# Attention and a gated feed-forward layer on one core: a written-out order of all tasks, other engines for some, and 32-column matmuls for one batch's kv

## The chip, the core and the metric

The kernel runs on one core of one Trainium2 chip. The metric is the time of one execution in device microseconds (us). The core has five engines that each work through their own list of instructions in order and wait for one another through semaphores: TensorE (PE in the profile, with its weight loads as PEld), VectorE (DVE), ScalarE (ACT), GpSimd (POOL) and SyncE (SP), whose queue issues the transfers here.

## What is computed

Four batches of attention with four heads, 1088 positions and 32 elements a head, by a polynomial feature map, then a normalized, gated feed-forward layer over all 4352 tokens:

```python
def phi(x):                                     # r = 8: 64 features of a head
    a = np.einsum('rd,bhsd->bhsr', S1, x)
    b = np.einsum('rd,bhsd->bhsr', S2, x)
    return np.einsum('bhsi,bhsj->bhsij', a, b).reshape(*x.shape[:-1], r * r)
q_p, k_p = phi(q), phi(k)
kv  = np.einsum('bhsf,bhsd->bhfd', k_p, v)      # one 64 x 32 matrix of a batch and head
z   = np.sum(k_p, axis=2)
num = np.einsum('bhsf,bhfd->bhsd', q_p, kv)
den = np.einsum('bhsf,bhf->bhs', q_p, z)[..., None] + 1e-06
x   = (num / den)                               # as 4352 tokens x 128
xn  = x / np.sqrt(np.mean(x * x, axis=-1, keepdims=True) + 1e-06) * rms_g
g, val = xn @ w_gate, xn @ w_val                # 128 -> 1536
out = g * (1 / (1 + np.exp(-g))) * val @ w_out  # 1536 -> 128
```

The weights and the sketch matrices S1 and S2 arrive as 64-bit floats, and the kernel converts them to 32 bits itself.

## The kernel before

**Tiling.** The 4352 tokens are cut into nine chunks, eight of 512 and one of 256. The 1536 hidden features are cut into twelve groups j of 128. A *slot* is one chunk and one j: gate product into `g_ps` and value product into `v_ps` (L786), silu on ScalarE (L795, tile `s`), their product `h` on VectorE (L798), and the product back to 128 features, added up in `o_ps` over the twelve j (L822, or L805 for the first four slots and the last two). Chunks 0 and 1 go through j in two halves each, chunks 2 to 8 in one pass. Slots are numbered t = 0 to 107 in that order.

**Split numbers.** TensorE multiplies rounded 32-bit numbers (fp32r) in one pass. So weights and activations are split in a rounded high and a rest: `w_hi`, `w_lo` (L494, L497), `x_hi`, `x_lo` (L738, L741), `h_hi` on ScalarE (L813) and `h_lo` on VectorE (L816). Each product is three matmuls. L805 multiplies exact 32-bit numbers instead, which takes no split. Attention's matmuls are exact too.

**Weights.** For each j, 384 KB are loaded into `w_raw` (L486) and converted by five steps on VectorE, the first of which may go to ScalarE (L426 to L445), then split. L497 may go to VectorE or GpSimd.

**Keys** (`kside`, one batch each): `kt` is multiplied with the sketch matrix `sblk` (L570), the 64 features of each head are formed as products (L528, L531; for one group of batch 0 on GpSimd, L513), and `kv` is added up over nine tiles of 128 positions (L580), with z as a 33rd column. Both use half of the array's columns: 64 columns of output to a matmul, in two column groups.

**Queries** (`qside`, one chunk each): features for chunks 0 and 1 as for the keys (L624, L531), then transposed (L632). For later chunks they are multiplied (L651), sent out to memory and read back spread (`at`, `bt`), and multiplied on VectorE (L677). Then numerators and denominators (L693), the division (L711, L712, L703), the mean square (`sq` on ScalarE, L715, with a scaling on VectorE, L725), its root on GpSimd (L728), scaling (L731 or L749), transposing (L735) and the split.

**What sets the order.** All of this is first collected as 1252 tasks in a plan: a task has the tiles that it reads and writes, and for each engine that may do it a cost in ns. `forward` (L231) then plays the engines through: at each step it takes the engine that can start earliest and, of its open tasks, the one with the lowest `late`, a number for each task from the table `LATE`. On TensorE a task gets 4000 on top if it changes between exact and rounded (`KIND`, L290). A task that two engines can do goes to the one that would finish it first. The instructions are written in the order of the start times that come out, and each engine works through its own in that order. Where TensorE would be idle for over 400 ns in that play, small warming matmuls are put in (L420).

Task numbers, which the new table uses, run in the order in which the code adds tasks: 0 to 7 the sketch matrix, 8 to 33 keys of batch 0 (with the first queries' load), 34 to 65 queries of chunk 0, 66 the load of chunk 1's, 67 to 186 weights, ten tasks a j, 187 to 204 keys of batch 1, 205 to 231 queries of chunk 1, then the slots, eleven tasks each for t = 0 and 1 (232 to 253), five for 2 and 3 and seven for later ones, with the keys of batches 2 and 3 and the queries of later chunks in between.

Of the kernel before, what the change touches and what calls it, by code (L numbers as in the profile page):

```python
# [19 lines left out]
R = 8  # L20
F = R * R
NT = B * S
P = 128
# [19 lines left out]
VPIECES = [(0, 5), (5, 9)]  # L43
K0 = [(0, 1), (1, 4), (4, 6), (6, 9)]
KN = [(0, 3), (3, 6), (6, 9)]
HOP = {"act": 36, "dve": 34, "pool": 80, "pe": 54, "dma": 60}
FIRST = 15000
LEADS = 1, 1.5, 2, 3, 4
EACHES = 2150, 2300, 2400
TELL = False  # L50
LATE = """
# [48 lines left out]
"""  # L100
LOOK = 250
MARGIN = 1500
KIND = 4000
WRAW = 7
POOL_K, POOL_Q = (1,), ()
LO_POOL, SCALED_ACT, PUT_ACT = 600, 100, 0
# [806 lines left out]
```

## Time and profile before

| | |
|---|---|
| Time, median of 3 runs | 272.04 us (271.98 to 272.32) |
| Profiled execution | 272.2 us, its span 270.0 us |
| Instructions | 4975 |
| TensorE busy | 263.7 us, 1842 matmul records |
| VectorE busy | 201.0 us, 383 |
| ScalarE busy | 162.1 us, 385 |
| GpSimd busy | 23.2 us, 37 |
| Granted TensorE clock | 1.000 |
| HBM read, written | 18.69 MB, 3.08 MB |

The span runs from the first to the last instruction. A matmul of exact 32-bit numbers shows as two records. Matmuls overlap in the array, so a row's mean duration is longer than the distance from one to the next; the chain of waits, which gives the time until the next piece begins, shows that distance. "x24" is a count.

### The profile page before, as it was taken

The numbers are of one execution on the slowest core, as the hardware profiler recorded it, in microseconds if no ns is written. First come the engines' busy times: TensorE is split into PE (matmuls) and PEld (weight loads), VectorE is DVE, ScalarE is ACT, GpSimd is POOL, SyncE is SP. The second block draws the span as 40 slices with busy tenths as digits, with TensorE's granted clock in tenths as the row PEclk, the third lists the DMA queues.
The fourth block names the chain that finished last, engine by engine and source line by source line (L and its number), as shares of the span: only waits on it lengthen the run. The fifth ranks groups of instructions, "written<-read, shape, count | busy, mean of one in ns | idle before, by whom it ended". The sixth has DMA issues, their size and how long they took to land.

```text
span 270.0 us, 4975 instructions
## 1 busy us (share of the span) xinstructions
PE 263.7 (98%) x1842; PEld 209.4 (78%) x1842; DVE 201.0 (74%) x383; ACT 162.1 (60%) x385; POOL 23.2 (9%) x37
## 2 busy tenths in 40 slices
PE   7899999999999999999999999999999999999995
PEld 4767687687788787778778787887777887887895
DVE  3799999999676786659646967678757755967582
ACT  4488796557554665717587556546646553855671
POOL 3132221230100010000100010001000100000000
PEclk9999999999999999999999999999999999999999
DMA  6999333041045001520016101610042001200100
GB/s 201 395 401 353 105 92 83 0 128 55 2 123 170 4 0 47 129 79 2 0 58 161 35 1 40 165 34 0 10 131 75 0 0 50 81 0 0 41 0 19
DMA packets 12087, 22.08 MB, mean 82 GB/s; under 512 B 1568, under 2 KB 3360, under 8 KB 12064
## 3 DMA queue, kind: packets, MB, share of 16 engines
q1 hardware_dynamic: 11920, 21.78, 25.5%
q8 instruction: 14, 0.23, 0.3%
q14 instruction: 9, 0.07, 0.1%
q10 hardware_dynamic: 144, 0.00, 0.0%
HBM read 18.69 MB, written 3.08 MB: 81 GB/s over the span
## 4 chain that ended last, share of the span: by engine, by line
PE 90%; DVE 4%; DMA 2%; ACT 1%; SPq 1%; issue 1%; POOL 0%; ACTq 0%
PE g_ps L786 26%; PE v_ps L786 26%; PE o_ps L822 24%; PE att L693 3%; PE att L580 3%; DMA vt<-v 2%; PE o_ps L805 2%; PE att L735 1%; PE att L651 1%; PE att L570 1%; PE o_ps L580 1%; DVE h L798 1%; DVE w_tmp L433 1%; DVE h_lo L816 0%; ACT h_hi L813 0%
## 5 line engine op out<-in xcount | busy, mean ns | idle before, releaser
L798 DVE TENSOR_TENSOR h<-v_ps,s 128x512 f32<-128x512 f32 (+2 forms) x109 | 70.1, 654 | 32.8 <-ACT s L795 16.1
L795 ACT ACTIVATE s<-g_ps 128x512 f32<-128x512 f32 (+1 forms) x108 | 60.2, 572 | 38.9 <-PE g_ps L786 21.6
L813 ACT CAST h_hi<-h 128x512 fp32r<-128x512 f32 (+1 forms) x102 | 59.5, 598 | 27.1 <-DVE h L798 23.0
L816 DVE TENSOR_TENSOR h_lo<-h,h_hi 128x512 fp32r<-128x512 f32 (+1 forms) x102 | 66.3, 667 | 10.4 <-ACT h_hi L813 9.0
L786 PE MATMUL g_ps<-x_hi,w_hi 128*128 128x512 f32 (+2 forms) x111 | 43.2, 389 | 0.0
L786 PE MATMUL v_ps<-x_hi,w_hi 128*128 128x512 f32 (+2 forms) x111 | 42.7, 384 | 0.0
L786 PE MATMUL g_ps<-x_hi,w_lo 128*128 128x512 f32 (+2 forms) x111 | 41.9, 378 | 0.4 <-DVE w_lo L497 0.4
L786 PE MATMUL v_ps<-x_lo,w_hi 128*128 128x512 f32 (+2 forms) x111 | 42.0, 378 | 0.0
L786 PE MATMUL v_ps<-x_hi,w_lo 128*128 128x512 f32 (+2 forms) x111 | 41.8, 377 | 0.0
L786 PE MATMUL g_ps<-x_lo,w_hi 128*128 128x512 f32 (+2 forms) x111 | 41.8, 378 | 0.0
L822 PE MATMUL o_ps<-h_hi,w_hi 128*128 128x512 f32 (+1 forms) x102 | 40.1, 393 | 0.0
L822 PE MATMUL o_ps<-h_lo,w_hi 128*128 128x512 f32 (+1 forms) x102 | 39.1, 383 | 0.0
L822 PE MATMUL o_ps<-h_hi,w_lo 128*128 128x512 f32 (+1 forms) x102 | 39.1, 383 | 0.0
L728 POOL TENSOR_TENSOR rstd<-ms,mhalf 128x4 f32<-128x4 f32 (+1 forms) x10 | 10.0, 1000 | 187.6 <-DVE ms L725 187.6
L786 PEld LDWEIGHTS g_ps<-x_hi,w_hi 128*128 128x128 f32 x111 | 20.9, 188 | 5.3 <-ACT s L795 0.6
L786 PEld LDWEIGHTS v_ps<-x_hi,w_hi 128*128 128x128 f32 x111 | 20.9, 188 | 4.6 <-DVE h L798 0.3
L786 PEld LDWEIGHTS g_ps<-x_hi,w_lo 128*128 128x128 f32 x111 | 20.9, 188 | 4.4 <-DVE w_lo L497 0.8
L786 PEld LDWEIGHTS v_ps<-x_lo,w_hi 128*128 128x128 f32 x111 | 20.9, 188 | 4.2
L786 PEld LDWEIGHTS g_ps<-x_lo,w_hi 128*128 128x128 f32 x111 | 20.8, 188 | 4.2
L786 PEld LDWEIGHTS v_ps<-x_hi,w_lo 128*128 128x128 f32 x111 | 20.9, 188 | 3.9
L822 PEld LDWEIGHTS o_ps<-h_hi,w_hi 128*128 128x128 f32 x102 | 19.2, 188 | 5.5 <-issue 1.3
L822 PEld LDWEIGHTS o_ps<-h_lo,w_hi 128*128 128x128 f32 x102 | 19.2, 188 | 4.1
(85 smaller groups left out, 257.8 us busy)
## 6 DMA issues: line engine op xcount, KB each, us to landing
w_raw<-w SPq DMA_DIRECT2D x12, 384.0 KB
bt<-far SPq DMA_DIRECT2D x24, 128.0 KB
at<-far SPq DMA_DIRECT2D x12, 256.0 KB
q<-qT SPq DMA_DIRECT2D x8, 256.0 KB
outT<-o_sb SPq DMA_DIRECT2D x8, 256.0 KB
vt<-v SPq DMA_DIRECT2D x4, 340.0 KB
kt<-kT SPq DMA_DIRECT2D x4, 320.0 KB
vt<-v SPq DMA_DIRECT2D x4, 272.0 KB
```

The lines of the kernel that those rows point to most:

```text
L433: nc.vector.tensor_scalar(out=u, in0=u, scalar1=5, scalar2=2, op0=ALU.logical_shift_left, op1=ALU.logical_shift_right)
L570: nc.tensor.matmul(out=ab()[hf * HALF:(hf + 1) * HALF, (t - lo) * HALF:(t - lo + 1) * HALF], lhsT=kt()[:, s0:s0 + HALF], rhs=sblk, start=T ...
L580: nc.tensor.matmul(out=kvv[rows, h // 2, :], lhsT=phi()[:, t, h * F:(h + 1) * F], rhs=vt()[:, t, h, :], start=(t == 0 and h < 2), stop=(t ...
L693: nc.tensor.matmul(out=nv[hf * HALF:(hf + 1) * HALF, t, p, :], lhsT=phi()[:, p, l0:l0 + HALF], rhs=kvs[(s0 + l0) // S][:, p, :], start=Tru ...
L728: nc.gpsimd.tensor_tensor(out=rstd()[:, us, 0], in0=ms()[:, us], in1=mhalf[:, us], op=ALU.pow)
L786: nc.tensor.matmul(out=acc()[:, cs], lhsT=wt[:, j, i3, :], rhs=x()[:, cs], start=(i == 0), stop=(i == 2))
L795: act(n, lambda: nc.scalar.activation(out=s()[:, :n], in_=gps()[:, :n], func=AF.Silu), cols(gps, whole[0]), [s])
L798: cs.stop - cs.start, lambda cs=cs: nc.vector.tensor_tensor(out=h()[:, cs], in0=vps()[:, cs], in1=s()[:, cs], op=ALU.mult),
L805: (cs.stop - cs.start) * 1.69, lambda cs=cs: nc.tensor.matmul(out=o_ps()[:, cs], lhsT=w_f[:, j, 2], rhs=h()[:, cs], start=first, stop=last ...
L813: act(n, lambda: nc.scalar.copy(out=h_hi()[:, :n], in_=h()[:, :n]), hs, [h_hi], True)
L816: eng.tensor_tensor(out=h_lo()[:, :n], in0=h()[:, :n], in1=h_hi().bitcast(F32)[:, :n], op=ALU.subtract)
L822: nc.tensor.matmul(out=o_ps()[:, :n], lhsT=wt[:, j, 2, :], rhs=x()[:, :n], start=first and i == 0, stop=last and i == 2,)
```

## The change

- `LATE` and the search over it are gone. `ORDER` lists all 1252 tasks in the order in which they are taken, and `ON` gives the engine of each of the 224 tasks that have two (a for ScalarE, d for VectorE, p for GpSimd). `follow` plays that order through once, only to get start times and warming matmuls.
- More tasks have two engines: copies out of the accumulators (ScalarE or VectorE), the feature products (VectorE or GpSimd), `at` times `bt` (the same), and `h_lo` (the same; 48 of 102 are given to GpSimd). For the products both factors are now copied out (`both`).
- The cost model no longer tells exact from rounded on TensorE but matmuls on part of the columns (`tiled`) from those on all, 95 ns at each change.
- The mean square is one VectorE instruction a tile (`tensor_tensor_reduce`), in place of a square on ScalarE and a scaling on VectorE.
- The gain vector comes as one more column of the first batch's keys, in place of a transfer of its own; each row of keys is one number longer.
- Batch 0's v comes in three loads in place of two, chunk 0's q in two in place of one. The first load of all is that of weight 0.
- kv of batch 2 (`QUARTERS`): each 64-column matmul becomes two of 32 columns, so that the outputs lie in four column groups.

The diff, cut to its core:

```diff
-LATE = """
--37035 -1206 -8314 1298 -10490 18870 15192 16396 -27501 -26844 -12692 -5713 -5435 -16853 4745 -3012 -1650 -18178 12804 -4772 -6470 -36037 -1883 12817
...
+ORDER = """
+67 68 69 70 11 0 12 1 4 2 3 5 6 39 40 8 34 16 71 66 72 20 35 9 41 13 205 21 7 22 210 73 77 17 36 42 14 18 211 24 15 28 75 25 206 297 74 37 207 212 26
+29 43 38 19 23 27 30 78 79 80 81 31 32 82 33 85 44 50 208 87 45 46 47 83 298 88 188 107 97 86 117 209 213 51 49 48 56 299 52 89 10 57 215 214 53 90 58
+55 59 187 301 476 221 54 300 61 91 216 62 92 236 60 592 232 217 63 127 84 98 237 233 218 247 243 248 147 64 234 190 99 219 238 65 235 307 93 100 240
...
+577 1057 578 560 286 462 552 833 1058 290 835 294 296 941 831 830 463 1059 464 295 942 944 470 943 471 605 611 583 650 626 472 579 553 554 584 561 585
...
+ON = (
+    "apadadaddaapaadaaadppappadpappappaddapdadpdppadpaddadpadddadddapaadaaddaapaddddaapdadddpdpadddddddppddpddddadadapdadddpp"
+    "dpdppdpaaddddpddppdpddpdaadpaddppdpppdpdddappappddpdppppdpddpddpddddpdpdppddddpapddpdpddppppddppdppppdda"
+)
+QUARTERS = (2,)
...
-SWITCH = 100
+SWITCH = 95
...
+    def follow(self, clock0, filler):
...
+        for i in map(int, ORDER.split()):
+            t = self.tasks[i]
+            e = t.on
...
             if e == "pe":
-                if exact and not w.exact:
+                if tiled != w.tiled:
                     occ, lat = occ + SWITCH, lat + SWITCH
-                exact = w.exact
+                tiled = w.tiled
...
+        copy(m * HALF, lambda: both()[:, :m * H], view, [ab], [both])
+        plan.add({
+            "dve": on_dve(m * H * F, lambda: outer(nc.vector, view())),
+            "pool": on_pool(m * H * F * 0.85, lambda: outer(nc.gpsimd, both()[:, :m * H]), PHI_POOL),
+        }, [ab, both], writes)
...
+            act(1, lambda: nc.scalar.copy(out=gain_t, in_=kt()[:, SP:]), [(kt, 1)], ["gain"], True)
...
                 kvv = acc()[:, :2 * VA].rearrange("p (a x) -> p a x", x=VA)
+                wide = F // 2 if b in QUARTERS else F
                 for t in range(lo, hi):
                     for h in range(H):
-                        rows = slice((h % 2) * F, (h % 2 + 1) * F)
-                        nc.tensor.matmul(
-                            out=kvv[rows, h // 2, :], lhsT=phi()[:, t, h * F:(h + 1) * F], rhs=vt()[:, t, h, :],
-                            start=(t == 0 and h < 2), stop=(t == KT - 1), skip_group_check=True,
-                        )
+                        for f in range(0, F, wide):
+                            r0 = (h % 2) * F + f
+                            nc.tensor.matmul(
+                                out=kvv[r0:r0 + wide, h // 2, :], lhsT=phi()[:, t, h * F + f:h * F + f + wide], rhs=vt()[:, t, h, :],
+                                start=(t == 0 and h < 2), stop=(t == KT - 1), skip_group_check=True,
+                            )
...
+                plan.add({
+                    "dve": on_dve(n, lambda times=times: times(nc.vector), True),
+                    "pool": on_pool(n, lambda times=times: times(nc.gpsimd), PHI_POOL),
+                }, [(at, p), (bt, p, 0), (bt, p, 1)], [(phi, "p", p)])
...
-                plan.add({"act": Way(300, 400, lambda t=t, u=u, sq=sq: nc.scalar.activation(
-                    out=sq()[:, t], in_=x()[:, u + t], func=AF.Square, accum_out=ss()[:, u + t:u + t + 1]
-                ))}, [(x, u)], [(sq, t), (ss, u + t)])
+                def mean(t=t, u=u, sq=sq):
+                    nc.vector.tensor_tensor_reduce(
+                        out=sq()[:, t], in0=x()[:, u + t], in1=x()[:, u + t], scale=1.0 / DM, scalar=EPS, op0=ALU.mult, op1=ALU.add,
+                        accum_out=ms()[:, u + t:u + t + 1],
+                    )
...
-            dve(n, lambda: low(nc.vector), [*hs, h_hi], [h_lo], lock=True)
+            plan.add({
+                "dve": on_dve(n, lambda: low(nc.vector), True), "pool": on_pool(n, lambda: low(nc.gpsimd), H_POOL)
+            }, [*hs, h_hi], [h_lo])
...
-    kT = np.zeros((B, H * D, SP), np.float32)
+    kT = np.zeros((B, H * D, SP + 1), np.float32)
```

More of the change, by code (lines that the diff above doesn't have):

```diff
@@ L138, in __init__ @@
         self.at, self.ways, self.deps, self.bufs, self.due = at, ways, deps, bufs, due
-        self.next, self.late, self.start, self.on, self.end = [], 0.0, None, None, None
+        self.next, self.late, self.start, self.on, self.end, self.only = [], 0.0, None, None, None, None
 class Plan:
@@ L204, in backward @@
-    def backward(self, lead, each):
-        for t in reversed(self.sorted()):
-            w = min(t.ways.values(), key=lambda w: w.occ + w.against)
-            e = next(k for k, v in t.ways.items() if v is w)
-            late = 1e9 if t.due is None else FIRST + each * t.due
-            for s in t.next:
-                to = next(iter(s.ways))
-                late = min(late, s.late - (w.occ if e == to == "pe" else lead * (w.lat + self.hop(e, to) + (FLIGHT + SETTLE if e == "dma" else 0))))
-            t.late = late
@@ L216, in sorted @@
-    def sorted(self):
-        left = {t: 0 for t in self.tasks}
-        for t in self.tasks:
-            for s in t.next:
-                left[s] += 1
-        out, todo = [], [t for t in self.tasks if not left[t]]
-        while todo:
-            t = todo.pop()
-            out.append(t)
-            for s in t.next:
-                left[s] -= 1
-                if not left[s]:
-                    todo.append(s)
-        return out
-    def forward(self, clock0, filler):
-        clock, out = dict(clock0), []
-        wire, port, landed, exact = 0, {"dve": 0, "pool": 0}, [], False
-        for t in self.tasks:
-            t.start = t.on = t.end = None
-        for row in self.rows.values():
-            for b in row:
-                b.live, b.left, b.until = False, len(b.tasks), 0
-        need = {t: len(t.deps) for t in self.tasks}
-        open_ = [t for t in self.tasks if not need[t]]
-        n = 0
-        users = {}
-        for t in self.tasks:
-            for d in t.deps:
-                users.setdefault(d, []).append(t)
-        def ready(t, e):
-            at = 0
+    def follow(self, clock0, filler):
+        clock, out, opened = dict(clock0), [], {}
+        wire, port, landed, tiled, stalls = 0, {"dve": 0, "pool": 0}, [], False, list(STALLS)
+        free = {id(row): [-1e9] * row[0].bufs for row in self.rows.values()}
+        many = iter(ON)
+        for t in self.tasks:
+            t.on = {"a": "act", "d": "dve", "p": "pool"}[next(many)] if len(t.ways) > 1 else next(iter(t.ways))
+        for i in map(int, ORDER.split()):
+            t = self.tasks[i]
+            e = t.on
+            w, at = t.ways[e], clock[e]
@@ L251, in ready @@
             for b in t.bufs:
-                if b.live:
-                    continue
-                before = b.row[:b.at]
-                if before and not before[-1].live:
-                    return None
-                held = sum(o.left > 0 for o in before[-3 * b.bufs:])
-                if held >= b.bufs:
-                    return None
-                if b.at >= b.bufs:
-                    done = sorted((o.until for o in before if not o.left), reverse=True)
-                    at = max(at, done[b.bufs - 1 - held] + HOP[e])
+                if b not in opened:
+                    opened[b] = [len(b.tasks), 0]
+                    row = free[id(b.row)]
+                    row.sort()
+                    at = max(at, row.pop(0) + HOP[e])
@@ L298, in forward @@
+            if e == "pe" and at - clock[e] > GAP:
                 k = int((at - clock[e] - SPARE) / UNIT)
@@ L330, in run @@
         self.clock0 = clock0
-        best = None
-        for lead, each in [(None, None)] if LATE.strip() else [(x, y) for x in LEADS for y in EACHES]:
-            if lead is None:
-                for t, x in zip(self.tasks, LATE.split(), strict=True):
-                    t.late = 20.0 * int(x)
-                self.arrange()
-            else:
-                self.links(lead, each)
-                self.backward(lead, each)
-            end, out = self.forward(clock0, filler)
-            if TELL:
-                print(lead, each, end)
-            if best is None or end < best[0]:
-                best = end, out, {t: (t.on, t.start, t.end, t.late) for t in self.tasks}
-        for t in self.tasks:
-            t.on, t.start, t.end, t.late = best[2][t]
-        for _, x in best[1]:
+        end, out = self.follow(clock0, filler)
+        for _, x in out:
             if isinstance(x, Task):
@@ L351, in run, with attention_then_glu @@
                 filler(x)
-        return best
+        return end, out, {t: (t.on, t.start, t.end, t.late) for t in self.tasks}
 @with_exitstack
-def attention_then_glu(ctx, tc, kT, v, qT, sw, w, gain, out):
+def attention_then_glu(ctx, tc, kT, v, qT, sw, w, out):
     nc = tc.nc
@@ L391, in load, with r3, copy @@
     def load(nbytes, emit, writes, reads=(), due=None):
-        plan.add({"dma": Way(ISSUE, nbytes / 330, emit)}, reads, writes, due)
+        plan.add({"dma": Way(ISSUE, nbytes / (385 if nbytes > 3000 * P else 320), emit)}, reads, writes, due)
+    def r3(n, passes=3):
+        return passes * max(110, 0.4453 * n + 4)
+    def copy(n, out, in_, reads, writes):
+        plan.add({
+            "act": on_act(n, lambda: nc.scalar.copy(out=out(), in_=in_())),
+            "dve": on_dve(n, lambda: nc.vector.tensor_copy(out=out(), in_=in_()), against=COPY_DVE),
+        }, reads, writes)
     ident = const.tile([P, P], F32, name="ident")
@@ L403, in attention_then_glu @@
         kvs.append(t)
-    gain_t = const.tile([P, 1], F32, name="gain_t")
-    nc.scalar.dma_start(out=gain_t, in_=gain)
     spare = const.tile([P, 4], F32, name="spare")
@@ L561, in kside @@
         for i, (lo, hi) in enumerate(groups):
-            m, ab = hi - lo, ps(("g_ps", "v_ps")[i % 2], 2) if first else ps("att", 3)
+            m, ab = hi - lo, gate(i % 2) if first or b == 1 and KEY1 else ps("att", ATT)
             if not i:
-                acc = ps("o_ps", 1) if first else ps("att", 3)
+                acc = ps("o_ps", 1) if first else ps("att", ATT)
             def mm(lo=lo, hi=hi, ab=ab):
                 for t in range(lo, hi):
-                    for hf in range(2):
-                        s0 = t * P + hf * HALF
+                    for rows in range(HALF), range(HALF, P):
+                        s0, n0 = t * P + rows.start, rows.start
                         nc.tensor.matmul(
-                            out=ab()[hf * HALF:(hf + 1) * HALF, (t - lo) * HALF:(t - lo + 1) * HALF],
-                            lhsT=kt()[:, s0:s0 + HALF], rhs=sblk, start=True, stop=True,
+                            out=ab()[n0:rows.stop, (t - lo) * HALF:(t - lo + 1) * HALF],
+                            lhsT=kt()[:, s0:s0 + len(rows)], rhs=sblk, start=True, stop=True,
                         )
@@ L603, in qload @@
         q = qs[c] = sb("q", [P, 512], 2)
-        load(P * n * 4, lambda: nc.sync.dma_start(out=q()[:, :n], in_=qT[:, s0:s0 + n]), [q])
+        for i, (lo, hi) in enumerate(((0, n // 2), (n // 2, n)) if not c and QHALVES else ((0, n),)):
+            load(P * (hi - lo) * 4, lambda lo=lo, hi=hi: nc.sync.dma_start(out=q()[:, lo:hi], in_=qT[:, s0 + lo:s0 + hi]), [(q, i)])
     def qside(c):
@@ L616, in qside @@
             for u in range(0, nt, 2):
-                ab = ps("att", 3)
-                tr = ps(("g_ps", "v_ps")[u // 2], 2) if first else ps("att", 3)
+                ab = ps("att", ATT)
+                tr = gate(u // 2) if first else ps("att", ATT)
                 def abmm(u=u, ab=ab):
@@ L743, in low @@
                 )
-            dve(5, mean, [(ss, i) for i in range(u, u + wd)], [(ms, u)], fast=True)
-            plan.add({"pool": Way(400 + 150 * wd, 430 + 150 * wd, root)}, [(ms, u)], [(rstd, u)])
+            plan.add({"pool": Way(400 + 150 * wd, 430 + 150 * wd, root)}, [(ms, i) for i in range(u, u + wd)], [(rstd, u)])
             def scaled_act(u=u, wd=wd):
@@ L824, in down @@
                     )
-            pe(n * 1.365, down, [h_hi, h_lo, ("w_hi", j, 1), ("w_lo", j, 1)], cols(o_ps, whole[0]), due, False)
+            pe(r3(n), down, [h_hi, h_lo, ("w_hi", j, 1), ("w_lo", j, 1)], cols(o_ps, whole[0]), due, False)
         if not last:
@@ L831, in slot @@
             part = parts[c] = sb("part", [P, 512], 2)
-            act(n, lambda: nc.scalar.copy(out=part()[:, :n], in_=o_ps()[:, :n]), done, [part])
+            copy(n, lambda: part()[:, :n], lambda: o_ps()[:, :n], done, [part])
             return
```

212 lines of the change are left out of this document (71 added, 141 removed), and 78 rows, old and new, of tables (LATE, ORDER).

## The prediction, made before the result was known

> **What bounds the kernel now.** I read the page first, then the busy time by stage, then the chain of waits in order of time. The page:
>
> ```profile
> span 270.0 us, 4975 instructions
> PE 263.7 (98%) x1842; PEld 209.4 (78%) x1842; DVE 201.0 (74%) x383; ACT 162.1 (60%) x385; POOL 23.2 (9%) x37
> PE 90%; DVE 4%; DMA 2%; ACT 1%; SPq 1%; issue 1%; POOL 0%; ACTq 0%
> ```
>
> TensorE is busy 98% of the span and carries 90% of the chain that ended last. By stage (columns: length, then busy time and count of PE, weight loads, DVE, ACT, POOL, then clock, DMA share, GB/s):
>
> ```profile
> 0.00:5.00 5.00, 4.22 (x32) 2.53 (x32) 0.92 (x6) 2.02 (x5) 1.30 (x10) 1.00 0.59 178
> 5.00:10.00 5.00, 3.79 (x93) 3.46 (x92) 3.70 (x7) 1.30 (x7) 1.51 (x1) 1.00 0.97 341
> 10.00:15.00 5.00, 4.73 (x82) 3.63 (x81) 4.20 (x14) 3.93 (x16) 1.65 (x3) 1.00 1.04 406
> 15.00:18.00 3.00, 2.34 (x19) 1.09 (x16) 2.73 (x7) 2.67 (x9) 1.92 (x3) 1.00 1.04 399
> 18.00:25.00 7.00, 7.00 (x76) 5.67 (x75) 6.58 (x17) 5.84 (x16) 0.78 (x2) 1.00 1.02 385
> 25.00:65.00 40.00, 39.55 (x285) 30.24 (x285) 39.25 (x76) 28.05 (x72) 8.98 (x13) 1.00 0.31 93
> 65.00:250.00 185.00, 185.00 (x1140) 146.58 (x1139) 133.33 (x234) 107.97 (x239) 7.02 (x7) 1.00 0.18 51
> ```
>
> Three regimes. Up to 18 us TensorE does warming matmuls and attention pieces while it waits for data. From 18 to 65 us it and VectorE are both full (VectorE 39.25 of 40 us). From 65 us on it is full and VectorE has 52 us to spare. The clock is 1.00 throughout. So the span can shrink in four ways: a shorter head, work brought into the head's holes, less TensorE time per piece, or fewer stalls. The arithmetic of the feed-forward slots is not touched.
>
> **Part 1: work brought ahead of slot 0.** The chain at the first slot (start, length in us, engine, tile, line):
>
> ```profile
> 2.60 5.01 DMA vt<-v
> 10.36 0.85 PE o_ps L580 x24
> 15.42 1.15 POOL rstd L728
> 16.59 0.41 ACT xn L749
> 17.05 0.62 PE att L735 x2
> 18.05 0.48 PE v_ps L786 x2
> 19.52 0.44 PE att L632 x4
> 19.95 0.38 PE att L624 x8
> 22.08 0.44 PE att L632 x4
> 22.52 0.62 PE att L693 x16
> 24.19 0.62 PE att L693 x16
> 30.93 0.58 PE att L651 x4
> ```
>
> The first slot's matmul starts at 18.05. Of chunk 1's query side one product (L624), both turns (L632), both numerators (L693) and chunk 2's product (L651) stand behind it, on the bound engine. In the new table, read with tasks numbered as the code adds them, these tasks (210, 208, 213, 215, 221, 298) all stand ahead of 236, the first slot matmul. The rows sum to 3.08 us with the cost of entering each stretch. Part 2 prices that entry; without it they are 0.44 + 0.23 + 0.44 + 0.46 + 0.46 + 0.43 = 2.5 us (29 ns a record for the narrow ones, part 2; 0.11 us a turn as it stands; L651 less 0.15). The cover is the head's idle and warming time: up to 18 us TensorE is idle 18 - 15.08 = 2.9 us, and warms during much of the rest. If that cover were gone the 2.5 us would move slot 0 instead. **-2.5 us.**
>
> Does slot 0 move? Two things push it back. The table issues a weight load (384 KB) and chunk 1's queries (256 KB) ahead of v; 640 KB at the 406 GB/s of the 10-to-15 row is 1.6 us. But v had landed at 7.61 and its last products ran only at 10.36, so 2.7 us of slack takes that. And VectorE does three steps of weight 0 ahead of the sketch matrix, each below the 0.59 us of L437 (part 4): up to 1.8 us on the way to kv, I take 1. One thing pulls forward: in the old chain the first half of slot 0 waits behind the second half's root (1.15), scaling (0.41) and turn. The table puts the first half's matmuls (236, 232) between the two turns (58, 63), about 1.2 us. The squares also leave ACT for one VectorE instruction each (34 of them); no row shows that form. Bounds: free, and the 0.31 us of a pair of them serially in the chain. I take **-0.15 us**, from -0.75 to +1.5.
>
> **Part 2: fewer stretches of narrow matmuls.** Attention's 64-column matmuls interrupt the full-width ones:
>
> ```profile
> 118.40 0.82 PE att L580 x24
> 121.52 1.52 PE att L580 x48
> 128.12 1.38 PE g_ps L786 x6
> 129.50 1.09 PE att L693 x32
> 130.59 1.60 PE v_ps L786 x6
> 246.72 0.62 PE att L693 x16
> ```
>
> From 24 to 48 records the price rises 0.70 us: 29 ns a record; the 24 cost 0.82, so entering costs 0.12 to 0.16 (32 records: 1.09 - 0.93). Six slot matmuls cost 1.38, but 1.60 right behind a narrow stretch: leaving costs 0.21. A stretch costs 0.35 us beside its work. Behind slot 0 the chain has 24 of them, from 19.95 to 246.72. In the table I count 11: the planner's penalty was on exact against rounded matmuls and is now on narrow against full width, and the narrow tasks stand in clumps (1057, 286, 462, 290, 294, 941, 470, 605, 611 follow one another on TensorE). 13 x 0.35 = **-4.55 us**. Nothing hides this: after 65 us TensorE has no idle. It is lost only if something else stalls it there.
>
> **Part 3: kv of the third batch.** Now 72 records of 64 columns: 72 x 29 ns = 2.1 us. After: 144 records of 32. A full-width turn costs 0.44/4 = 0.11 us a record, so 64 columns alone should cost 0.055; 29 ns says two column groups run side by side. If four do, a record costs about 7 ns and all of it 1.05 us: -1.05. If only two do, 0. If the price sits on the record, 144 x 29 = 4.2: +2.1. In the table these tasks stand between 64-column ones; changing between 64 and 32 columns occurs as two round trips, at nothing or at 0.35 each as for full width. I take the first with both trips, **-0.35 us**, ends -1.05 and +2.8. [...] No row here changes between 64 and 32.
>
> **Part 4: VectorE and POOL, up to 65 us.**
>
> ```profile
> L437 DVE SCALAR_TENSOR_TENSOR w_tmp<-w_raw,w_tmp 128x384 uint32<-128x384 uint32 x12 | 7.0, 587 | 0.2
> L440 DVE SCALAR_TENSOR_TENSOR w_f<-w_raw,w_tmp 128x384 uint32<-128x384 uint32 x12 | 7.2, 596 | 0.1
> 16.56 0.96 DVE L437 SCALAR_TENSOR_TENSOR w_tmp<-w_raw,w_tmp 128x384 uint32<-128x384 uint32 x1
> 16.39 0.72 POOL L497 TENSOR_TENSOR w_lo<-w_f,w_hi 128x256 fp32r<-128x256 f32 x1
> L816 DVE TENSOR_TENSOR h_lo<-h,h_hi 128x512 fp32r<-128x512 f32 (+1 forms) x102 | 66.3, 667 | 10.4 <-ACT h_hi L813 9.0
> L715 ACT ACTIVATE sq<-x 128x128 f32<-128x128 f32 x34 | 10.1, 300 | 8.1 <-DVE x L703 7.9
> L725 DVE TENSOR_SCALAR ms<-ss 128x4 f32<-128x4 f32 (+1 forms) x10 | 1.7, 166 | 3.7 <-ACT sq L715 3.7
> L677 DVE TENSOR_TENSOR phiq<-at,bt 128x512 f32<-128x512 f32 (+1 forms) x14 | 8.9, 648 | 1.5 <-DMA at<-far 0.9 <-issue 0.5
> L531 DVE TENSOR_TENSOR phn<-att,bs 128x512 f32<-128x512 f32 x4 | 2.7, 688 | 0.3 <-ACT bs L528 0.2
> ```
>
> To be 3.2 us ahead at 65 us (2.5, and two stretches fewer by then, 0.7) TensorE needs VectorE ahead as well. VectorE was idle 18 - 11.55 = 6.45 us before 18 us; the table starts weight 0 as soon as it lands, which I estimate wins 1.7 of it (three steps up to 0.59 before the sketch matrix, as above). POOL takes from it two outer products (2 x 0.69), in this stretch three h_lo (3 x 0.65) and two products of at and bt (2 x 0.65). Fourteen square sums come to it (14 x 0.3, the ACT row's mean as the nearest) and a copy of about 0.3; five scalings (L725) leave, 0.8. That is 1.7 + 1.4 + 1.9 + 1.3 - 4.2 - 0.3 + 0.8 = 2.6 of the 3.2. Then POOL's hold: the 0.96 us step above ran beside the POOL instruction below it and took 0.4 more than its mean of 0.587. By the table POOL has some 20 tasks in this stretch where the rows of 18 to 65 us have 15; five more at half a hold (0.2) are 1.0, of which I keep 0.8. Stalls: 3.2 - 2.6 + 0.8 = **+1.4 us**, from 0 to 5. Behind 65 us the 45 other h_lo on POOL hide in VectorE's 52 spare us.
>
> Edits at nothing: the gain vector inside the first key load (it was one ACT-queue transfer, needed only at x_hi), v in three loads and the first q in two (more issues on SP's queue, which ends with nobody waiting), copies that may go to either engine (ACT is at 60%). Each key row is 4 bytes longer; if its loads were slower the keys after batch 0 have tens of us of slack.
>
> **Sum**, against the profiled execution (272.2 us, span 270.0, so 2.2 around it; the median of the runs, 272.04, is 0.16 lower): -2.5 - 0.15 - 4.55 - 0.35 + 1.4 = -6.15. Span 263.85, time 266.05, say 266.0.
>
> **Rivals.**
> - *VectorE paces the start.* For it: 39.25 of 40 us. All 3.2 us won up to 65 us are then lost and the holds with them, 4.0 instead of 1.4: 268.65. Against it: the h_lo and the products moved away.
> - *The price sits on the record.* Part 3 is +2.1 + 0.7 instead of -0.35: 269.2. For it: 34, 64 or 66 moving columns all cost 29 to 31 ns, so what is streamed isn't the bound. Against: 29 ns is below a fair share of one column group. [...]
> - *POOL holds VectorE, slower than before.* [...] A 512-column h_lo would be twice the 0.72 us row's 256, 1.4 us. Where VectorE is full, 20 tasks at 0.45 us are 9.0 instead of 0.8: 274.2. It turns slower than before at holds of 0.35 us a task on average (0.8 + 6.2 over 20). Against it: the hold seen is 0.4 on one task, and the steps that read PSUM aren't held.
> - *No change:* the clumps make TensorE wait for a late producer by about what they save, 6 us over 11 clumps: 272. The clumps' inputs stand far ahead in the table, so I give it little.
>
> **Chances.** Forecast 0.60 (its own range 263.0 to 268.0), VectorE paces 0.18, the record 0.12, POOL 0.06, no change 0.04. About 0.2% (0.5 us) is what a measurement of this kernel can tell from no change. The first three are faster: 0.90; same 0.04; slower 0.06. Low end: part 3 at -1.05, slot 0 at -0.75 and stalls at 0.1 give 272.2 - 8.75 = 263.4, and a little below for a shorter tail: 263.0. High end: the record case with its stalls 1 us worse, 270.2; what is left out is 0.10 and the tails.
>
> **What would show it.** Right: in the chain, the first slot matmul near 17.9 us with no L632, L693 or query product of chunk 1 behind it; 11 narrow stretches behind it; kv of batch 2 at 144 records in about 1.1 us; TensorE idle or waiting about 2 to 3 us between 18 and 75 us; span near 264. Wrong: slot 0 behind 19 us; kv of batch 2 over 3.5 us; w_lo, h or h_lo as releaser of TensorE for more than 5 us; VectorE steps of 0.8 us and more in large number.

## The result, and the profile after

The changed kernel takes 269.09 us in the median of nine executions (267.24 to 270.51), the kernel before 272.04 (271.92 to 272.32): a ratio of 0.988 (95% interval 0.985 to 0.991). The prediction was 266.0. The sign was right; the time lies inside the whole range (up to 270.2) but outside the forecast's own (263.0 to 268.0), and the gain is 2.95 us where 6.04 was forecast. The page:

```profile
span 265.9 us, 5090 instructions
PE 258.7 (97%) x1898; PEld 207.7 (78%) x1898; DVE 183.6 (69%) x396; ACT 147.3 (55%) x315; POOL 94.9 (36%) x94
PE 84%; DVE 7%; DMA 4%; ACT 1%; issue 1%; POOL 1%; SPq 0%; DVEq 0%
```

TensorE is still the bound and GpSimd has the work that VectorE and ScalarE gave up. By stage:

```profile
10.00:12.00 2.00, 1.41 (x35) 1.08 (x33) 1.42 (x3) 0.48 (x2) 1.10 (x2) 1.00 0.94 336
12.00:14.00 2.00, 1.47 (x40) 1.36 (x40) 1.49 (x3) 1.27 (x3) 0.00 (x0) 1.00 1.04 413
14.00:16.00 2.00, 0.92 (x30) 0.92 (x32) 1.38 (x5) 0.93 (x4) 0.34 (x1) 1.00 1.02 398
...
105.00:150.00 45.00, 44.38 (x481) 36.26 (x480) 30.46 (x66) 21.94 (x43) 17.53 (x14) 1.00 0.18 47
```

Two places show where the forecast gain went. TensorE is idle for 0.5 to 1.1 us in each 2 us between 10 and 16 us, just ahead of the first slot. And it loses 0.62 us between 105 and 150 us, where it was full before. The chain of waits (start, length, what) names both:

```profile
13.31 0.37 DVE w_tmp L314
...
13.70 0.37 DVE w_tmp L318
...
14.10 0.56 DVE w_tmp L322
14.65 0.14 DVE kv L463
...
14.82 0.22 ACT kv L467
...
15.08 0.71 PE att L569 x16
...
17.31 0.91 POOL rstd L604
...
20.14 0.44 PE v_ps L661 x2
...
105.08 0.56 PE att L452 x44
105.64 0.50 PE att L440 x12
106.14 1.06 PE att L452 x89
107.20 0.58 PE att L523 x4
107.78 0.43 PE att L440 x12
...
108.23 0.62 issue
108.86 1.15 PE att L569 x31
```

The numerators of chunk 0 (L569; "nmm" from here on) start at 15.08. In the chain they stand behind three conversion steps of weight 1 on VectorE. Before, they started at 11.77 (L693; in brackets, in all timelines here: idle before it, and why):

```profile
11.77 1.16 PE L693 MATMUL att<-kv,phiq 128*64 128x66 f32 x32 [0.27 <-ACT kv L595]
```

After, VectorE had waited earlier too, for a turn on TensorE ahead of chunk 1's second product, with two key products queued behind it:

```profile
10.42 0.69 DVE L397 TENSOR_TENSOR phn<-att,both 128x512 f32<-128x512 f32 x1 [1.35 <-PE g_ps L505]
```

At 108.23 TensorE waits for nothing that the profile names ("issue").

To judge the prediction by its steps I read two moments from each trace: the start of slot 0's first matmul and the end of the last matmul. Between them lies what I call the body.

| kernel (profiled execution) | nmm starts | slot 0 starts | last matmul ends | body | clock |
|---|---|---|---|---|---|
| before | 11.77 | 18.03 | 267.08 | 249.05 | 1.000 |
| after | 15.08 | 20.07 | 262.82 | 242.75 | 1.000 |
| after, again | 15.16 | 21.05 | 263.76 | 242.71 | 0.994 |

Profiled, the body is 6.30 us shorter (predicted 6.0), and slot 0 starts 2.04 us later (predicted 0.15 earlier). The rest of the miss is in the clock. The kernel before ran at a granted clock of 0.998 or more nearly always; fourteen executions of the changed one, the five of the first experiment among them, divide like this:

| granted clock | executions | us |
|---|---|---|
| 1.000 | 4 | 267.24 to 267.86 |
| 0.994 | 6 | 268.29 to 269.09 |
| 0.987 | 4 | 269.44 to 270.51 |

So the median lies 1.4 us over the profiled execution (267.71), which ran at full clock.

### The profile page after: what moved, and what is told of

Its sections match the earlier page's. It is cut to its first block, busy times and chain, and to the rows that moved or that the text cites. A ratio compares the mean times of both kernels' runs of the same rounds, so it can differ in the third digit from the quotient of the medians.

```text
span 265.9 us, 5090 instructions
## 1 busy us (share of the span) xinstructions
PE 258.7 (97%) x1898; PEld 207.7 (78%) x1898; DVE 183.6 (69%) x396; ACT 147.3 (55%) x315; POOL 94.9 (36%) x94
## 4 chain that ended last, share of the span: by engine, by line
PE 84%; DVE 7%; DMA 4%; ACT 1%; issue 1%; POOL 1%; SPq 0%; DVEq 0%
PE v_ps L661 24%; PE g_ps L661 24%; PE o_ps L699 24%; PE att L569 3%; PE att L305 2%; DMA vt<-v 2%; DMA bt<-far 2%; DVE h L673 2%; PE att L452 1%; PE att L440 1%; PE att L611 1%; PE o_ps L680 1%; DVE w_lo L382 1%; DVE h_lo L691 1%; PE att L523 1%
## 5 line engine op out<-in xcount | busy, mean ns | idle before, releaser
L691 POOL TENSOR_TENSOR h_lo<-h,h_hi 128x512 fp32r<-128x512 f32 (+1 forms) x48 | 60.8, 1275 | 104.8 <-ACT h_hi L688 87.1
L688 ACT CAST h_hi<-h 128x512 fp32r<-128x512 f32 (+1 forms) x102 | 58.7, 598 | 26.9 <-DVE h L673 21.2
L691 DVE TENSOR_TENSOR h_lo<-h,h_hi 128x512 fp32r<-128x512 f32 (+1 forms) x54 | 41.5, 781 | 10.4 <-ACT h_hi L688 10.2
L661 PE MATMUL v_ps<-x_hi,w_hi 128*128 128x512 f32 (+2 forms) x111 | 43.4, 391 | 0.2 <-DVE h L673 0.2
```

The lines of the kernel that those rows point to most:

```text
L661: nc.tensor.matmul(out=acc()[:, cs], lhsT=wt[:, j, i3, :], rhs=x()[:, cs], start=(i == 0), stop=(i == 2))
L688: act(n, lambda: nc.scalar.copy(out=h_hi()[:, :n], in_=h()[:, :n]), hs, [h_hi], True)
L691: eng.tensor_tensor(out=h_lo()[:, :n], in0=h()[:, :n], in1=h_hi().bitcast(F32)[:, :n], op=ALU.subtract)
```

## Experiments

Numbers in `ORDER` are task numbers; a diff shows the stretch of the table that moves. 31 is batch 0's last kv product, 32 and 33 are kv's evictions, 78 to 82 the five steps of weight 1, 212 chunk 1's second feature product, 44 the first numerator (nmm).

**1. The changed kernel again**, no edit.

> The changed kernel again, nothing edited, to see whether its executions always spread (267.2 to 270.5 so far) or settle. Theory (a lower granted clock makes the spread): each execution's time follows its granted clock, about 267.6 at 1.000, 268.7 at 0.994, 269.8 at 0.987, and the median again lies at 268.5 to 269.8; where the profile falls on an execution below 1.000, the slices with a granted clock under full speed lie in the first 25 us. Rival (chance in the DMA landings makes the spread): executions of equal clock differ by 1 us or more.

Measured 268.64 us (267.42 to 268.97, five executions; ratio 0.986, 0.984 to 0.988). The profiled one ran at 0.994, and its stages show where:

```profile
14.00:16.00 2.00, 0.84 (x16) 0.84 (x18) 1.30 (x4) 0.85 (x4) 0.26 (x1) 0.64 1.02 401
16.00:18.00 2.00, 2.00 (x26) 1.71 (x24) 1.56 (x10) 0.42 (x1) 0.29 (x2) 0.51 0.21 81
18.00:20.00 2.00, 1.91 (x26) 1.17 (x24) 1.66 (x8) 1.79 (x6) 1.54 (x2) 1.00 0.04 8
```

The clock (the column behind GpSimd's busy time, ahead of the DMA share) falls to 0.51. The trace's clock records give the edges: full speed from 4.32 us, half from 14.56 to 17.97. That is three stretches of 3.413 us (I call such a stretch a window) and then one at half. In the traces of the kernel before and of the changed one the clock is full from 4.48 us for 266.24 us and from 6.78 us for 259.41: 78 and 76 windows, whose edges lie elsewhere in each trace. In the window ahead of the drop TensorE's matmuls cover 54% of the time. Slot 0 starts 0.98 us later, and the body is the same. The clock thus orders the executions, as the first theory has it: those of equal clock lie within 0.6 us at 1.000 and 0.8 at 0.994. The four at 0.987, all among the first nine, are 1.1 apart, which the rival asked for; so the clock isn't all of the spread.

**2. kv's eviction ahead of weight 1's steps.**

```diff
-29 43 38 19 23 27 30 78 79 80 81 31 32 82 33 85 44 50
+29 43 38 19 23 27 30 78 79 31 32 80 81 82 33 85 44 50
```

> Only the order of VectorE's queue ahead of slot 0 changes: batch 0's last kv product and the first kv eviction stand in the table ahead of the last w1 steps (c and e) instead of behind them. Theory (the late start of slot 0 is kv's eviction behind VectorE's weight steps): nmm starts 0.6 to 0.8 us earlier than 15.08, slot 0 starts at 19.2 to 19.5 instead of 20.07, and the end moves as much: 266.9 to 267.1 at a clock of 1.0. Rival (kv's own data is what is late, or VectorE's total of work up to 60 us paces): the first nmm moves by under 0.3 us, or slot 0 moves and the end stays within 0.2 us of 267.7 at a clock of 1.0.

Measured 268.81 us (268.57 to 269.99). nmm starts at 14.53, 0.55 earlier, a little under what was expected. All five executions ran at 0.994 or less, and the profiled one at half clock from 13.77 to 20.60, two windows. The planner had also put two warming matmuls at 17.75, 1.0 us at half clock, which the changed kernel doesn't have, and slot 0 came at 22.41. At 0.994 the times equal the changed kernel's, so the half microsecond gained at nmm doesn't show at the end; with the clock and the warming matmuls in between, this run can't say what it is worth. The body is 242.79: it doesn't change when slot 0 moves back by 2.3 us, which VectorE has as a head start. So VectorE doesn't pace the body here.

**3. More fillers (warming matmuls), in the shared bank.**

```diff
+MORE_WARM = {27: 1, 44: 5, 213: 1, 221: 1}
...
             if isinstance(x, Task):
+                if x.at in MORE_WARM:
+                    filler(MORE_WARM[x.at])
                 x.ways[x.on].emit()
```

> Eight more 128x128 filler matmuls on TensorE, put where it stands idle in the first 20 us (one ahead of the third kv task of batch 0, five ahead of the first nmm, one ahead of each of two tasks of chunk 1's queries). Theory (idle stretches of TensorE in the head let the granted clock fall in most executions): every execution shows 1.000 and 267.3 to 268.2, the median about 267.7, 1.4 us under the changed kernel's. Rival (the clock falls elsewhere, or whatever the head does): the same spread over 1.000, 0.994 and 0.987 and a median of 268.5 to 270; the fillers themselves cost 0 to 0.9 us if they delay nmm.

Measured 269.97 us (269.75 to 270.52), clock 0.999 or 1.000 in all four executions. So the fillers hold the clock, but the time went up by 2.3 us at equal clock: nmm started at 14.99, slot 0 only at 21.75. The fillers write one of the accumulator banks that take turns under the name `att`, which the numerators use too, and the profile shows TensorE idle twice in between, 0.59 and 0.67 us, where the changed kernel flowed. So a warming matmul isn't free wherever TensorE stands idle. That the shared bank is the cause is not shown: run 5, with banks of their own, also leaves out two of the places.

**4. kv of the third batch with 64 features again.**

```diff
-QUARTERS = (2,)
+QUARTERS = ()
```

> Part 3 undone alone: kv of the third batch again with 64 features to a matmul, two column groups, the order table as it is. Theory of the prediction (quarters save 0.35 us: 1.05 from four column groups, less 0.7 for two changes between 64 and 32 columns): 0.35 us slower. Rival (the stall of 0.6 to 0.8 us at 108 us, behind the dense run of small matmuls, comes from the quarters' count of instructions): the kv matmuls cost 1.05 us more, the changes fall away (about 0.26, two of 0.13) and the stall of 0.6 to 0.8 with them, so that it ends within 0.2 us of the changed kernel at equal clock.

Measured 268.01 us (267.15 to 268.59); body 242.09, so 0.66 us *shorter* without the quarters. Neither number was met: the prediction had the undoing 0.35 slower, the rival had it even. The chain:

```profile
105.92 0.37 PE att L523 x4
106.29 0.67 PE att L452 x24
106.96 0.38 PE att L440 x12
107.33 1.38 PE att L452 x48
108.71 0.46 PE att L523 x4
109.17 0.35 PE att L440 x12
```

kv costs 0.67 + 1.38 here and 0.56 + 1.06 with quarters (144 records of 32: the timeline has x48 and x96, of which x44 and x89 are on the chain): the four column groups do save 0.43. The neighbours (L440, L523) are 0.32 cheaper without the changes between 64 and 32 columns, and the "issue" is gone. Undoing the quarters thus costs 0.43 and saves 0.32 + 0.62, which is most of the 0.66; the numerators behind the stall took 1.15 us in the changed kernel and take 0.94 here.

**5. Fillers in banks of their own.**

```diff
             def kvmm(lo=lo, hi=hi):
...
+                for _ in range(2 if first and lo == 4 else 0):
+                    nc.tensor.matmul(out=acc()[:1, 256:256 + P], lhsT=zeros[:, :1], rhs=zeros, start=True, stop=True, skip_group_check=True)
...
             def nmm(u=u, num=num):
+                for _ in range(5 if first and not u else 0):
+                    nc.tensor.matmul(out=num()[:1, :P], lhsT=zeros[:, :1], rhs=zeros, start=True, stop=True)
```

The two fillers in kv's bank start a new sum there, so part of batch 0's kv is left out of this kernel's result; the work done is the same.

> Seven fillers (128x128, to one column) on TensorE that write into banks the waiting task owns already: two ahead of the third kv task of batch 0, five ahead of the first nmm. Theory (a window of 3.41 us in which TensorE does little, 10 to 15 us after the start, halves the clock for the next window, and where the windows lie differs by execution): clock 1.000 in every execution, slot 0 at 20.0 to 20.3, from there to the last matmul 242.7 as in the runs so far, so 267.3 to 268.0 in every execution. Rival (the fillers that shared the att bank cost 1.7 us by delaying slot 0, and any filler there does): slot 0 at 21 us or later, 268.5 or more.

Measured 267.78 us (267.23 to 268.24), clock 0.998 to 1.000 in six of six executions, against four of fourteen without. Slot 0 starts at 20.16. The first theory holds: thin work of TensorE between 10 and 15 us costs the clock, and about 1.3 us in the median. The body was 0.5 longer than expected (243.26): the "issue" at 107.73 had grown to 1.25 us. Fourteen more records ahead of it should not matter, unless the stall depends on the *count* of instructions. The next two runs ask that.

**6. Quarters in all four batches.**

```diff
-QUARTERS = (2,)
+QUARTERS = (0, 1, 2, 3)
```

> kv of all four batches with 32 features to a matmul, not only of the third. Read from slot 0's first matmul to the last matmul, which was 242.75 us in the changed kernel and 242.09 with 64 features everywhere. [...] Theory B (the stall at 108 us belongs to what stands there): no stall in batches 1 and 3, the body 241.8 to 242.1.

Measured 271.48 us (270.19 to 272.90), body 243.32, over theory B's range. If the count of instructions makes the stall, batches 1 and 3 should each show a new one. The timeline of TensorE in batch 0's last kv product, batch 1's kv and batch 3's:

```profile
14.96 0.41 PE L452 MATMUL o_ps<-vt,phi 128*32 128x34 f32 x26 [1.80 <-issue]
...
45.13 0.63 PE L452 MATMUL att<-vt,phi 128*32 128x34 f32 x48
46.28 0.94 PE L452 MATMUL att<-vt,phi 128*32 128x34 f32 x85
48.38 0.32 PE L452 MATMUL att<-vt,phi 128*32 128x34 f32 x11 [1.17 <-issue]
...
129.78 0.63 PE L452 MATMUL att<-vt,phi 128*32 128x34 f32 x48
130.97 1.04 PE L452 MATMUL att<-vt,phi 128*32 128x34 f32 x96
131.93 0.50 PE L661 MATMUL g_ps<-x_hi,w_hi 128*128 128x512 f32 x1
```

Batch 1 has a new stall of 1.17 us, inside its kv, with nothing of nmm near. Batch 3 has none and gains: its stretch takes 2.15 us where it took 2.69. So the count alone holds for one of the two and fails for the other. Batch 0, in quarters too, has the longest stall, 1.80 us ahead of slot 0: nmm starts at 15.95 and slot 0 at 22.06, and that, more than the body, is why this run is slower than the changed kernel. The profile's list of DMA queues has what I read as the reason:

```profile
q8 instruction: 15, 0.25, 0.4%
```

(From the changed kernel: packets, MB, share.) In the trace each of the fifteen packets has 16,384 bytes, 0.25 MB together; 1898 matmuls and as many weight loads would be 65 bytes each. So I read q8 as TensorE's instructions and estimate some 250 to a packet: 3796 over 15 are 253, and from one packet's start to the next the trace has 242 matmuls and weight loads on average, that of the kernel before 244. The count of packets moves with TensorE's records, 14 with 1826 (run 4) and 16 with 2114 (this run). In the trace a packet starts at 106.27 in the changed kernel, and the stall ends at 108.86; here packets start at 12.48, 45.43 and 124.63, and the stalls end at 14.96 and 48.38. In all traces with a stall it is 2.2 to 3.0 us from the start of a packet until TensorE goes on, and 250 instructions of quarters, at two a record and 10 ns a record, are by estimate used up in about 1.3. In batch 3 the packet had started 5.15 us ahead of kv's first matmul (129.78); in the changed kernel's trace a packet takes 0.9 to 1.4 us.

**7. The dense run spread.** Four tasks (1057, 286, 462, 290) stand four wide tasks earlier:

```diff
+1057 286 462 290
...
-577 1057 578 560 286 462 552 833 1058 290 835 294 296 941 831 830 463 1059 464 295 942 944 470 943 471 605 611
+577 578 560 552 833 1058 835 294 296 941 831 830 463 1059 464 295 942 944 470 943 471 605 611
```

> Only the order: four tasks of the dense run at 105 us (chunk 8's sums, the first two kv products of batch 2, the first key sum of batch 3) stand four 512-wide tasks earlier, which makes one more narrow stretch. Theory A (loading of instructions): the stall of 0.8 us at 108 us falls away, the extra stretch costs 0.35, the body is 242.2 to 242.4 against 242.75. Theory B (the stall belongs to the product nmm that stands behind it): it stays, and the body is 243.0 to 243.2.

Measured 267.64 us (266.64 to 268.80; ratio 0.983, 0.978 to 0.987), 266.64 and 267.08 at full clock. Body 242.02, even under A's range, and no "issue" piece between 100 and 121 us:

```profile
102.01 0.56 PE att L452 x44
...
103.07 0.56 PE att L452 x44
...
106.62 0.56 PE att L452 x44
107.18 0.58 PE att L523 x4
107.76 0.35 PE att L440 x12
```

The stall went although nmm stayed where it was and one stretch was added. Runs 4, 6 and 7 thus agree with theory A; that the packets are the cause is read from their times.

**8. Seven stretches more.** Of seven groups of neighbouring narrow tasks, the last or the last two stand some five wide tasks later. One of them, as TensorE takes its tasks (489, 283 and 495 are narrow):

```diff
-489 283 495 428 422 398 399 376
+489 283 428 422 398 399 376 495
```

> Only the order: seven of the narrow tasks behind slot 0 (two key sums, a kv product twice, sums and products of chunks 3, 4, 5 and 7) stand four to six wide tasks later than their neighbours, so that there are 18 narrow stretches behind slot 0 instead of 11. Theory (part 2: each change between full and narrow matmuls and back costs 0.35 us): the body grows by 7 times 0.35, 2.45 us, from 242.75 to about 245.2. Rival (the gain came from the other parts, and the stretches hide under waits): the body grows by under 1 us.

Measured 277.34 us (276.05 to 278.67), body 248.41: more than twice the growth expected. Its profiled execution ran at half clock from 16.78 to 27.02, into the slots, the planner had put in a warming matmul at 38 us, and a key sum waited 0.5 us. The clean part is behind 85 us: from the 198th of 986 slot matmul records to the last end it takes 188.56 us against 186.99, with four stretches more, 0.39 each (0.42 without the "issue" of each, 0.52 here and 0.62 there). One of the split ones in the chain:

```profile
76.57 0.62 PE att L569 x16
77.19 0.89 PE o_ps L699 x3
78.08 1.40 PE v_ps L661 x6
79.47 0.69 PE o_ps L699 x3
```

Sixteen records at 29 ns are 0.46, so entering costs 0.16; three slot matmuls cost 0.89 behind it and 0.69 elsewhere, so leaving costs 0.20. Part 2's price stands; the head's growth is not explained in full.

**9. Keys first, weight 1 behind.**

```diff
-77 17 36 42 14 18 211 24 15 28 75 25 206 297 74 37 207 212 26 29 43 38 19 23 27 30 78 79 80 81 31 32 82 33 85 44 50
+17 36 42 14 18 211 24 15 77 28 75 25 206 297 74 37 207 26 29 43 38 19 23 27 30 212 31 32 33 78 79 80 81 82 85 44 50
```

> Only the order ahead of slot 0: on VectorE the two last key products of batch 0 stand ahead of chunk 1's second query product (which waits 1.4 us for a turn on TensorE, with the key products queued behind it), kv's last product and its evictions stand ahead of all of w1's steps, and w1's load stands behind the load of v's last piece. Theory (slot 0 came 2 us later than predicted because batch 0's kv is held up there): nmm starts at 12.8 to 13.6 instead of 15.1, slot 0 at 17.8 to 18.6 instead of 20.07, the body stays 242.75, so 265.3 to 266.3 at a clock of 1.0. Rival (w1's steps and chunk 1's turn, now later on VectorE, take kv's place): nmm earlier by over 1 us, slot 0 still behind 19.3.

Measured 270.99 us (269.91 to 273.16). nmm starts at 13.27, as expected, and slot 0 at 21.58: the rival. VectorE's timeline:

```profile
12.76 0.22 DVE L463 COPY kv<-o_ps 64x66 f32<-64x66 f32 x1 [0.40 <-PE o_ps L452]
13.84 0.36 DVE L314 TENSOR_SCALAR w_tmp<-w_tmp 128x384 f32<-128x384 f32 x1 [0.86 <-ACT w_tmp L330]
...
15.23 0.56 DVE L325 SCALAR_TENSOR_TENSOR w_f<-w_raw,w_tmp 128x384 uint32<-128x384 uint32 x1
15.70 0.16 DVE L586 TENSOR_SCALAR den<-att 128x8 f32<-128x8 f32 x1
```

The denominators could start at about 13.9, 0.6 us of numerators behind 13.27, and stand behind weight 1's steps until 15.70. The next turn on TensorE started only at 16.70, and the planner had put six warming matmuls, 1.5 us, behind it. The wait moved from kv to the divisions. The body is 243.90, 1.15 us longer than expected: 0.6 of it is in batch 1's kv at 45 us, where a key product on VectorE ends at 47.14 and TensorE's next kv record starts at 47.20, and 0.3 is a longer "issue" at 110 us (0.94).

**10 and 11. Keys first with fillers and the spread, quarters in batches 2 and 3; and with 64 everywhere.** The table of 9; one warming matmul ahead of task 27, three in the bank of the first nmm as in 5; 10 has the move of 7 and `QUARTERS = (2, 3)`, 11 `QUARTERS = ()`.

> Keys first as in the run before, with fillers (one ahead of the third kv task, three in the bank of the first nmm), the spread order of batch 2's kv, and 32 features to a matmul in batches 2 and 3. Theory, by the parts: slot 0 at 17.8 to 18.6, body 242.02 with the spread order, less 0.5 for batch 3, no stall of instructions: 241.5, so 264.1 to 265.0, and a clock of 1.0 in nearly all executions. [...]

> Keys first with the same fillers, and 64 features to a matmul in all batches. Theory: no dense run overtakes the loading of instructions, body 242.1 as with 64 features before, slot 0 at 17.8 to 18.6, 264.6 to 265.6 at a clock of 1.0. If it is within 0.3 us of the kernel with quarters in two batches, the four column groups are worth nothing here, stall or none; by the theory it is 0.5 us slower.

Measured 269.36 (267.87 to 270.26) and 270.10 us (269.04 to 271.61); slot 0 at 21.73 and 23.98, for the reason that 9 showed (the second with half clock from 19.14 to 22.55), and three of six executions of each at 0.994. The bodies are 242.33 and 242.83, 0.50 apart as expected, and neither shows the "issue": in two batches and without the stall, the four column groups are worth half a microsecond, one stretch more included. Both bodies are 0.7 to 0.8 longer than the parts add up to; 0.6 of that is in batch 1's kv at 45 us, which takes 3.71 us instead of 3.11, as in 9.

**12. On VectorE, what slot 0 waits for goes first.** With it go the fillers of 10, its move and its `QUARTERS`, and the planner's warming matmuls behind 9 us are left out.

```diff
-207 212 26 29 43 38 19 23 27 30 78 79 80 81 31 32 82 33 85 44 50 208 87 45 46 47 83
+207 26 29 43 38 19 23 27 30 212 78 31 32 33 79 80 44 50 208 87 45 46 47 49 48
...
+53 55 54 81 82
...
+60 89 90 91 92
...
-            else:
+            elif _ < 9000:
                 filler(x)
```

> On VectorE ahead of slot 0 the work that slot 0 waits for goes first: the key products, kv's evictions and the division and mean of chunk 0's rows stand ahead of w1's last two steps (1.1 us) and of all four steps of w2 (1.8 us); the loads keep their order. With it the spread order of batch 2's kv, 32 features in batches 2 and 3, a filler ahead of the third kv task and three in the first nmm's bank, and no planned filler after the first 9 us. Theory (VectorE's queue, not its total, sets the start of slot 0): nmm at 13.0 to 13.8, slot 0 at 17.6 to 18.8, body 241.5 to 242.2, so 263.6 to 265.5 at a clock of 1.0. Rival (VectorE's total paces the start: what is put behind comes due at slots 1 and 2): slot 0 earlier by over 1 us, but the body longer by as much, 265.5 to 267.5; or slot 0 not before 19.5.

Measured 267.61 us (266.83 to 270.62; ratio 0.986, 0.982 to 0.990). nmm at 13.32, slot 0 at 18.22, and from nmm to slot 0 4.90 us, as in the changed kernel (4.99): the earlier start is nmm's, and comes from VectorE's *order*. But the body is 243.81, and the waits of TensorE behind 12 us (line numbers four higher than in the changed kernel) are led by one (total, times, longest us):

```profile
PE g_ps L665 <- DVE x_lo L621: 1.4, 1, 1.4
```

```profile
18.58 0.28 DVE w_tmp L316
...
18.89 0.37 DVE w_tmp L320
...
19.28 0.98 DVE w_tmp L324
...
20.28 0.70 DVE w_f L327
```

Weight 2's steps, 2.4 us of them, now stand ahead of the second half of chunk 0's rest (`x_lo`). Of the 1.85 us won at slot 0, 1.4 came back as one wait. By the numbers this is the rival (265.5 to 267.5; the four executions at 0.998 or more took 266.83 to 267.78): the work put behind came due at once. Whether another order of the same work would keep more is open.

Run 7 beats both kernels on its median, as 12 does, and, at full clock, by 0.2 to 1.2 us the changed one, which its body's 0.73 explains; the intervals of the two ratios overlap. The table of 7 with fillers like those of 5 and nothing else was not tried.

## Why the prediction was right, and where it wasn't

The miss of 3.1 us in four pieces: slot 0's start +2.2, the body -0.3, what lies at the end and around the span -0.2 (the tail 0.07 longer, 1.86 around the span and not 2.16), the clock +1.4. That the whole range held is luck: its upper end was drawn for a price per record and for VectorE, and neither slot 0's 2 us nor the clock was in it. The forecast's own range did not hold.

- **Does slot 0 move? (-0.15 us) failed.** It started at 20.07 and not near 17.9, past the bound of 19 that the text set for itself. The forecast pull of 1.2 us was there: from nmm to slot 0 took 4.99 us instead of 6.26. But nmm started 3.31 us later, where I had given VectorE's new steps 1 us. I priced three steps of weight 0 and not the whole queue: chunk 1's second product stood ahead of two key products and waited 1.35 us for a turn, and weight 1's steps stood ahead of kv's eviction. kv's last product ended at 13.78 (11.18 before), and its eviction started only at 14.57. Work brought ahead of slot 0 brought its VectorE steps with it. Runs 9 and 12 show this for 1.8 of the 3.31 us: with the key products and evictions ahead, nmm starts at 13.3. No run takes the other 1.5 us apart.
- **The clock was taken as given.** "The clock is 1.00 throughout" was read off the kernel before. TensorE's cover of the head got thinner in the change (26 warming records instead of 42), and ten of fourteen executions ran at a lower granted clock; the one of them with a trace (run 1) shows a window at half clock. Runs 3 and 5 show it: with fillers in the thin stretch all ten executions keep 0.998 or more. No long gap announced the drop in run 1: the longest idle gap of TensorE by it was 1.3 us, and half of it lay in the window ahead.
- **Parts 1 and 2 (-2.5, -4.55) held together.** All six tasks stand ahead of slot 0, eleven stretches are left, at 0.33 to 0.37 us each; run 8 puts 0.39 on each stretch added. Of the body's -6.30, part 3 is +0.66 and part 4 -0.2 (below), so -6.8 is left for these two, where -7.05 was forecast. How it divides between them is not measured.
- **Part 3 (-0.35) had the wrong sign.** From 48 to 96 records of 32 columns the chain takes 0.50 us more, 10 ns a record against 29 for 64 columns, which I read as four column groups at once; and kv saved 0.43, where 1.05 was forecast (it takes 1.62 us, not about 1.1). The changes on the neighbours took 0.32, less than the 0.7 paid for them. What failed is this size, and that nothing was counted for the "issue" behind kv, 0.62 us, by the reading of run 6 the supply of instructions; by run 4 the whole part is +0.66. The rival "the price sits on the record" was wrong in its price and right that more records are not free.
- **Part 4 (+1.4) was too high.** The text looked for 2 to 3 us of TensorE idle between 18 and 75 us. From slot 0 to 75 us it is 0.27, and it was 0.45 before: -0.2. So the body came out right to 0.3 us in part by luck, part 4 being 1.6 too high and part 3 1.0 too low. That the body is the same with slot 0 at 20.1, 21.05 and 22.4 speaks against VectorE pacing it. With kv brought forward it does: by 0.6 us at 45 us in runs 9 to 11, and by the 1.4 us of run 12, with slot 0 at 18.2. The rival "VectorE paces the start" was thus at work in the changed kernel ahead of slot 0, and not, as it was put, by a loss behind it.
- **POOL holds VectorE** did not decide: h_lo on VectorE rose from a mean of 667 ns to 781, but the ten up to 70 us took 679 to 693 ns; what rose lies behind, where VectorE has time to spare. No run shows the rival's 0.45 us on each of 20 tasks. What the changed kernel's trace shows: of 13 h_lo of 512 columns on VectorE beside an h_lo or a product of POOL, ten took 842 to 1768 ns and three 681 to 693, as the other 37 did (679 to 693); `h`, which reads an accumulator, took at most 694 ns in all 36 such cases.

## What to carry to other kernels

When work is pulled ahead into idle time of the bound engine, follow what each helper engine's queue then looks like at the point where the critical step stands, in order and with its releasers, not by adding up steps. Many short matmuls in a row met a count here as well as a time: by the reading of run 6 some 250 TensorE instructions come in one packet, and TensorE went on 2.2 to 3.0 us after the start of the next. And a change that thins out the bound engine's first microseconds can cost the clock in some executions only, here ten of fourteen, so a single profile doesn't show it.

## What the hardware showed that I had not expected

- The clock fell to half for 3.41 us (runs 1 and 11), 6.83 (run 2) and 10.24 (run 8), one to three windows. It fell behind windows in which TensorE's matmuls covered about half the time or less: 54, 45, 26, 49 and 42% in runs 1, 4, 6, 8 and 11. Windows covered to 58 to 64% were followed by full clock in six traces (both kernels', runs 2, 3, 7 and 10). Yet in run 2 a window covered to 74%, by kv's 34-column matmuls almost alone, was followed by half clock, and one of the same cover and the same matmuls was not in the changed kernel's profile. Which measure decides is open.
- Stalls of 0.35 to 1.25 us that no semaphore explains, in eight traces of eight with the dense run of quarters whole, none in the five with it spread or at 64 columns. Their size moves with the number of records ahead: 0.62 and 0.35 in the two traces of the changed kernel, 0.94 to 1.25 with twelve to sixteen records more (runs 3, 5 and 9). Run 6 has two more in its other batches, 1.80 and 1.17 us.
- 32-column matmuls in four column groups go at 10 ns a record (48 more in 0.50 us, changed kernel), 64-column ones in two groups at 29 (24 more in 0.70 us, kernel before).
